# V mixed one column at a time: an attention-plus-feed-forward kernel on one Trainium2 core

## The chip, the cores and the metric

The kernel runs on one core of one Trainium2 chip. The metric is the device time of one execution in microseconds (us); of the kernel before, three runs are shown, with a median of 286.13 us (286.0 to 287.14). Engines are named as in the profile: PE is TensorE's matmul side and PEld its weight loads, DVE is VectorE, ACT is ScalarE, POOL is GpSimd, and SP is SyncE, which here only issues transfers. A matmul reads two operands from SBUF: the weights (`lhsT`), which are loaded first, and the moving operand (`rhs`), which is streamed past them. Both have the summed dimension on the partitions. The result has the weights' columns on its partitions and the moving columns along its rows, and lands in PSUM, from where DVE or ACT copies it to SBUF (an "eviction").

## What is computed

Four batches, 8 heads, 768 positions, 64 numbers per head; the positions form 8 blocks of 96. A small matrix per head, `sort_net` (8x8), is normalised five times over rows and columns, and then mixes the blocks of K and V. Attention is inside a block. The result goes through a gated feed-forward layer (512 to 1536 to 512).

```python
for _ in range(5):
    P = P - np.max(P, axis=-1, keepdims=True)
    P = np.exp(P)
    P = P / (np.sum(P, axis=-1, keepdims=True) + 1e-09)
    P = P / (np.sum(P, axis=-2, keepdims=True) + 1e-09)
k_sorted = np.einsum('bhij,bhjcd->bhicd', P, k_b)
v_sorted = np.einsum('bhij,bhjcd->bhicd', P, v_b)
scores = scale * (q_b @ k_sorted^T)          # per block of 96
attn = softmax(scores)
x = (attn @ v_sorted), heads side by side     # 3072 x 512
out = (silu(x @ w_gate) * (x @ w_val)) @ w_out
```

Here `j` is the block that is read, `i` the block that results, `c` the position in a block (96), `d` the number in a head (64). The attention needs, for each head and block `i`, the mixed V with its keys `c` on the partitions: that is the tile `vt` (96 partitions, 64 pairs of head and block, 64 numbers).

## The kernel before

The work is cut into 8 units: half a batch each, 4 of the 8 blocks of all heads, 384 rows of the result. A unit's attention goes by pairs of heads (`hp`, four per unit): `qk` (scores, tile `s`), `rowmax`, `shift`, `expo`, `rowsum`, `norm` (tile `en`), `turn` (the normalised weights are transposed on PE, tile `et`), `av` (they meet `vt`, and the result is evicted to `xt`). A unit's feed-forward has 12 steps: `ffn_up` (two times 4 matmuls, `g_ps` and `u_ps`, and a tanh on ACT), `ffn_gate` (DVE), and `ffn_down` of the unit before (`o_ps`, 3 of 12 matmuls per step). The feed-forward of a unit overlaps the attention of the next one.

Preparation, once per batch: Q is transposed on PE in 3 pieces (`q_piece`), K is mixed and transposed in 6 (`k_piece`, by `mix_t`), V is mixed in 6 (`v_piece`).

The order is written out by hand. Each step is put into a list with a due time in feed-forward steps, the list is sorted, and each engine runs its instructions in that order; a step that waits holds up whatever stands behind it on its engine. `prep` (L366) gives the due times of the pieces: batch 1's fall into the feed-forward of unit 0, batch 2's and 3's into that of the units 1, 2 and 3, 4. For the first unit there is a list of its own (`first`, L399), which runs ahead of all feed-forward steps.

V takes two ways:

- Batch 0: `load_v` puts V on 128 partitions, 16 per head: block `j` and half `ch` of the block, with 48 positions of 64 numbers along the row. `v0_piece` mixes it as `k_piece` mixes K: 6 pieces of 16 matmuls, of 64 weight columns (the numbers `d` at one position) and 64 moving columns (from `bdk`, a block-diagonal form of the mixing matrix). That leaves `d` on the partitions (`vT`). `v0_turn` then transposes on PE: 8 groups of 4 transposes (`vt_ps`), each evicted by ACT. The six pieces and eight turns are spread over `first` and the steps right behind it.
- Batches 1 to 3: `v_piece` is one matmul with `bdk` as weights and 512 moving columns of V, so the mixed V has head, block and half on the partitions (tile `vm`). `v_turn` writes it to a scratch tensor in DRAM with a transfer issued by SP and reads it back with keys on the partitions with a second one, in runs of 128 bytes. SP also issues the stores of the result.

All pieces of a batch after the first use the PSUM tag "m", a ring of two buffers shared with `turn` and `av`; the first unit's use "up", a ring of three, later used by `g_ps` and `u_ps`. ACT evicts all pieces of batches 1 to 3.

`bdk` comes out of the normalised matrix so: `spread_p` multiplies a 0/1 selection (`selk`) with it, which repeats each head's rows on its 16 partitions; `make_zk` keeps each partition's own column with a mask (`mjk`) and a sum; `make_bdk` spreads the outcome into the block-diagonal form with a second mask (`m1`). The masks are made on DVE and POOL during the five rounds. Loads of Q, K, V and the weights are issued by POOL (`load_q`, `load_k`, `load_v`, `load_w`) and convert to bf16 on the way.

```python
nc.tensor.matmul(ps.rearrange("p c d -> p (c d)"),          # v_piece
                 lhsT=bdk[:, b].rearrange("p h i c -> p (h i c)"),
                 rhs=vn[b][:, ts(n, 8), :].rearrange("p c d -> p (c d)"))
```

The functions that the change touches and what calls them, with the line numbers that the profile uses:

Of the kernel before, what the change touches and what calls it, by code (L numbers as in the profile page):

```python
# [9 lines left out]
FP32 = mybir.dt.float32  # L10
BF16 = mybir.dt.bfloat16
AF = mybir.ActivationFunctionType
ALU = mybir.AluOpType
AX = mybir.AxisListType
# [3 lines left out]
def kernel(  # L18
# [8 lines left out]
    moe_w_out: bass.AP,  # L27
    out: bass.AP,
):

    nc = tc.nc

    B, H, S, D = q.shape
    NB = sort_net.shape[-1]
# [12 lines left out]
    CH = 2  # L55
# [11 lines left out]
    hpool = ctx.enter_context(tc.tile_pool(name="hpool", bufs=2))  # L67
    gsp = ctx.enter_context(tc.tile_pool(name="gsp", bufs=3))
    opool = ctx.enter_context(tc.tile_pool(name="opool", bufs=3))
    dramp = ctx.enter_context(tc.tile_pool(name="dramp", bufs=2, space=bass.MemoryType.DRAM))  # L70
    psum = ctx.enter_context(tc.tile_pool(name="psum", bufs=2, space=bass.MemoryType.PSUM))

    def ps_tile(shape, dt, name, tag):
        return psum.tile(shape, dt, name=name, tag=tag, bufs={"up": 3, "o": 1, "s": 1, "m": 2}[tag])
# [17 lines left out]
        nc.gpsimd.dma_start(out=qn[b], in_=src)  # L92

    def load_v(b):
        vn[b] = natp.tile([128, CK, D], BF16, name="vn", tag="vn", bufs=2)
        src = v[b].rearrange("h (j ch c) d -> (h j ch) c d", j=NB, ch=CH)
        nc.gpsimd.dma_start(out=vn[b], in_=src)

    def load_w(dst, w, f0, f1):
        src = w.rearrange("(x hp d) f -> x d hp f", x=2, hp=HP)  # L100
# [17 lines left out]
    def evict(eng, dst, src):  # L118
        if eng == "act":
            nc.scalar.copy(dst, src)  # L120
        else:
            nc.vector.tensor_copy(dst, src)
# [11 lines left out]
    def mix_t(nat, b, dst, n, eng, tag):  # L134

        ps = ps_tile([128, 8, 64], FP32, "k_ps", tag)
        for l in range(8):
            for x in range(2):
                nc.tensor.matmul(ps[ds(64 * x, 64), l, :], lhsT=nat[:, n * 8 + l, :],  # L139
                                 rhs=bdk[:, b, ds(HP * x, HP)].rearrange("p a i c -> p (a i c)"),  # L140
                                 start=True, stop=True)
        dst = dst.rearrange("p hp i (ch c) -> p (hp i ch) c", ch=CH)
        evict(eng, dst[:, :, ts(n, 8)], ps.transpose([0, 2, 1]))
# [3 lines left out]
            tr["k", b] = trp.tile([128, HP, NB, BLK], BF16, name="kt", tag="kt")  # L147
        mix_t(kn[b], b, tr["k", b], n, eng, tag)

    def v0_piece(n, eng, tag):  # L150

        if n == 0:
            tr["vT"] = natp.tile([128, HP, NB, BLK], BF16, name="vT")
            tr["v", 0] = trp.tile([BLK, H * NB, D], BF16, name="vt", tag="vt")
        mix_t(vn[0], 0, tr["vT"], n, eng, tag)

    def v0_turn(hp, half, eng, tag):
        ps = ps_tile([BLK, HB, 2, D], BF16, "vt_ps", tag)
        for i in range(HB):
            nc.tensor.transpose(ps[:, i].rearrange("p x d -> p (x d)"),  # L160
                                tr["vT"][:, hp, half * HB + i, :], ident)
        dst = tr["v", 0].rearrange("p (x hp i) d -> p hp i x d", x=2, hp=HP)
        evict(eng, dst[:, hp, ds(half * HB, HB)], ps)

    def v_piece(b, n, eng, tag):
        if n == 0:
            tr["vm", b] = natp.tile([128, CK, D], BF16, name="vm", tag="vm", bufs=2)
        ps = ps_tile([128, 8, D], FP32, "v_ps", tag)
        nc.tensor.matmul(ps.rearrange("p c d -> p (c d)"),
                         lhsT=bdk[:, b].rearrange("p h i c -> p (h i c)"),  # L170
                         rhs=vn[b][:, ts(n, 8), :].rearrange("p c d -> p (c d)"),
                         start=True, stop=True)
        evict(eng, tr["vm", b][:, ts(n, 8), :], ps)

    def v_turn(b):
        scr = dramp.tile([H * NB, BLK, D], BF16, name="vscr", tag="vscr")
        nc.sync.dma_start(out=scr.rearrange("hi (ch c) d -> (hi ch) c d", ch=CH), in_=tr["vm", b])
        tr["v", b] = trp.tile([BLK, H * NB, D], BF16, name="vt", tag="vt")
        nc.sync.dma_start(out=tr["v", b], in_=scr.rearrange("hi c d -> c hi d"))


    nc.vector.memset(p_sb[:, NB:NB + 1, :], 1e-9)
    P = p_sb[:, 0:NB, :]
# [5 lines left out]
    for it in range(N_ITER):  # L189
        nc.scalar.activation(P, P, AF.Exp)  # L190
        nc.vector.reduce_sum(rowred[:, :, 0], P, axis=AX.X)
        nc.vector.reciprocal(rowred, rowred)
        nc.vector.tensor_mul(P, P, rowred.to_broadcast([BH, NB, NB]))
        nc.vector.reduce_sum(colred[:, 0, :], p_sb.transpose([0, 2, 1]), axis=AX.X)
        nc.vector.reciprocal(colred, colred)
        nc.vector.tensor_mul(pbf if it == N_ITER - 1 else P, P,
                             colred.to_broadcast([BH, NB, NB]))
        if it == N_ITER - 2:
            q_piece(0, 0, "act", "m")
        if it == N_ITER - 1:  # L200
            q_piece(0, 1, "act", "m")
            q_piece(0, 2, "act", "o")
        if it == 0:

            selk = const.tile([BH, BH, 16], BF16, name="selk")
            nc.gpsimd.tensor_copy(selk, ident[0:BH, 0:BH].unsqueeze(2).to_broadcast([BH, BH, 16]))
        if it == 1:
            mjk = const.tile([128, 1, NB], FP32, name="mjk")
            nc.vector.reduce_sum(mjk[:, 0, :], ident.rearrange("p (h j ch) -> p j h ch", j=NB, ch=CH),
                                 axis=AX.XY)  # L210
        if it == 2:
            m1 = const.tile([128, 8, CH], FP32, name="m1")
            nc.vector.reduce_sum(m1, ident.rearrange("p (h j ch) -> p h ch j", j=NB, ch=CH), axis=AX.X)


    zkr = const.tile([128, B, NB], FP32, name="zkr")
# [2 lines left out]
    def spread_p(b0, b1):  # L219
        ps = ps_tile([128, b1 - b0, NB, NB], FP32, "zk_ps", "up")  # L220
        for b in range(b0, b1):
            nc.tensor.matmul(ps[:, b - b0].rearrange("p i j -> p (i j)"),
                             lhsT=selk[:, ds(b * H, H), :].rearrange("p h r -> p (h r)"),
                             rhs=pbf.rearrange("p i j -> p (i j)"), start=True, stop=True)
        return ps

    def make_zk(b0, b1, ps):
        n = (b1 - b0) * NB
        zk = const.tile([128, n, NB], FP32, name=f"zk{b0}")
        nc.vector.tensor_tensor(zk, ps.rearrange("p b i j -> p (b i) j"),  # L230
                                mjk.to_broadcast([128, n, NB]), op=ALU.mult)
        nc.vector.reduce_sum(zkr[:, b0:b1, :].rearrange("p b i -> p (b i)"), zk, axis=AX.X)

    def make_bdk(b, eng):
        eng.tensor_tensor(
            bdk[:, b],
            m1.unsqueeze(2).to_broadcast([128, H, NB, CH]),
            zkr[:, b, :].unsqueeze(1).unsqueeze(3).to_broadcast([128, H, NB, CH]),
            op=ALU.mult)
# [120 lines left out]
    def at(t, f, *args):  # L360
        steps.append((t, lambda: f(*args)))
# [2 lines left out]
        nc.gpsimd.dma_start(out=wo_sb, in_=moe_w_out.rearrange("(mc p) f -> p mc f", p=128))  # L364

    def prep(b, tv, tk, tq, *engs):  # L366

        n = 0
        for f, times in [(v_piece, tv), (k_piece, tk), (q_piece, tq)]:
            for i, t in enumerate(times):  # L370
                at(t, f, b, i, engs[n % len(engs)], "m")
                n += 1
        at(tv[-1] + 0.3, v_turn, b)

    T0 = -15.6
    load_v(1)
    load_k(1)
    zk_ps = spread_p(0, 1), spread_p(1, B)
    make_zk(0, 1, zk_ps[0])
    make_bdk(0, nc.vector)  # L380
    for n in range(6):
        k_piece(0, n, ("dve", "act")[n % 2], ("m", "up", "m", "up", "m", "o")[n])
    make_zk(1, B, zk_ps[1])
# [4 lines left out]
    load_q(1)  # L388


    def v0(*ns):
        for n in ns:
            v0_piece(n, "act", "up")

    def vx(half, *hps):
        for hp in hps:
            v0_turn(hp, half, "act", "up")

    first = [(qk, 0), (rowmax, 0), (v0, 0, 1, 2), (shift, 0), (expo, 0), (qk, 1), (rowmax, 1),  # L399
             (v0, 3, 4), (shift, 1), (expo, 1), (v0, 5), (rowsum, 0), (norm, 0), (qk, 2),  # L400
             (rowmax, 2), (vx, 0, 0, 1), (shift, 2), (expo, 2), (rowsum, 1), (norm, 1),
             (vx, 0, 2, 3), (qk, 3), (turn, 0), (rowmax, 3), (shift, 3), (expo, 3), (av, 0),
             (turn, 1), (rowsum, 2), (norm, 2), (av, 1), (rowsum, 3),
             (norm, 3, (nc.vector, nc.gpsimd)), (vx, 1, 0, 1)]
    for f, *args in first:
        f(*args) if f in (v0, vx) else f(0, *args)
    at(T0 + 11.9, turn, 0, 2)
    at(T0 + 12.15, av, 0, 2)
    at(T0 + 12.7, turn, 0, 3)
    at(T0 + 13.0, av, 0, 3)  # L410
    at(T0 + 13.05, vx, 1, 2, 3)

    at(0.1, load_wo)
    at(2.1, load_v, 2)
# [2 lines left out]
    at(15.1, load_v, 3)  # L417
    at(17.1, load_k, 3)
    at(19.1, load_q, 3)
    prep(1, [0.45 + 0.5 * n for n in range(6)], [3.45 + 0.6 * n for n in range(6)],  # L420
         [7.2, 8.0, 8.8], "act")
    for b in range(2, B):
        t = 24 * (b - 2) + 12.45
        prep(b, [t + n for n in range(6)], [t + 6 + n for n in range(6)],
             [t + 12 + 2 * n for n in range(3)], "act")
    for u in range(1, NU):
        steps += att_steps(u, 12 * u + T0 + (u == 2))
# [39 lines left out]
```

## Time and profile before

| what | value |
|---|---|
| median of the runs shown | 286.13 us (286.0, 286.13, 287.14) |
| the profiled execution: span from its first to its last instruction | 284.0 us |
| PE busy | 258.5 us (91%) |
| DVE busy | 204.0 us (72%) |
| ACT busy | 164.3 us (58%) |
| POOL busy | 70.3 us (25%) |
| V, batch 0: `vT` matmuls (L139), turns (L160) on PE | 3.0 and 4.1 us |
| V, batch 0: evictions of `vT` and `vt` on ACT | 3.2 and 4.3 us |
| V, batches 1 to 3: 18 matmuls (L169), 18 evictions to `vm` | 6.8 and 10.4 us |
| V, batches 1 to 3: DRAM trip, issue to landing, medians | 6.7 out, 8.3 back |

The page gives, for the profiled execution, the busy time of each engine, the busy tenths in 40 slices of 7.1 us, the transfers, the chain of work that ended last, and the costliest groups of instructions. Of the execution's own time the profile has the span only; the median of the runs is 2.1 us longer. In a group, "busy" is the time in which at least one of its instructions ran and "mean ns" is that of one, so for overlapping matmuls the mean is longer than the distance between two starts. How long PE needs for a group is read from the order of time instead: the start of the next group less its own.

### The profile page before, as it was taken

How to read it: one execution, taken by the hardware profiler on the slowest of the kernel's cores; microseconds unless marked ns; L12 is line 12 of the kernel's file. 1: busy time of each engine (PE TensorE's matmuls, PEld its weight loads, DVE VectorE, ACT ScalarE, POOL GpSimd, SP SyncE). 2: the span in 40 equal slices, each digit the busy share in tenths (PEclk: the TensorE clock that was granted, in tenths of full speed). 3: DMA queues.
4: the chain of work that ended last, by engine and by line, in shares of the span. 5: the costliest groups of instructions: out<-in, count | busy, mean ns of one | idle time of the engine just before them, and what ended most of it. 6: DMA issues, size and time to landing. Idle time of an engine off the chain costs nothing.

```text
span 284.0 us, 6237 instructions
## 1 busy us (share of the span) xinstructions
PE 258.5 (91%) x2550; PEld 154.6 (54%) x2550; DVE 204.0 (72%) x360; ACT 164.3 (58%) x291; POOL 70.3 (25%) x98
## 2 busy tenths in 40 slices
PE   0577789989999999999999999999999999999983
PEld 0566645655556665555555655555555555555531
DVE  5789577749778777888887777888888887556500
ACT  2568779885766767546666666554555445432311
POOL 8155362433332222222211222222222222000000
PEclk9955589999999999999999999999999999999999
DMA  6999999997399911001039100101000010000021
GB/s 105 216 206 221 204 203 197 268 207 75 51 227 244 111 39 38 10 31 39 28 137 133 39 2 37 40 0 39 38 37 2 37 39 37 18 22 37 37 76 74
DMA packets 28412, 25.57 MB, mean 90 GB/s; under 512 B 19296, under 2 KB 22880, under 8 KB 28384
## 3 DMA queue, kind: packets, MB, share of 16 engines
q0 software_dynamic: 5968, 14.16, 26.7%
q1 hardware_dynamic: 22416, 11.02, 15.9%
q8 instruction: 20, 0.33, 0.5%
q14 instruction: 8, 0.07, 0.1%
HBM read 30.68 MB, written 8.65 MB: 138 GB/s over the span
## 4 chain that ended last, share of the span: by engine, by line
PE 65%; DVE 15%; ACT 12%; issue 4%; DMA 2%; DVEq 0%; ACTq 0%; POOLq 0%
PE o_ps L346 19%; PE g_ps L318 17%; PE u_ps L318 14%; DVE e L262 5%; DVE rm L257 5%; PE av_ps L298 3%; ACT et L120 3%; PE k_ps L139 3%; ACT e L267 3%; PE et_ps L285 2%; DMA qn<-in_q_dram 2%; ACT th L328 2%; PE s L251 2%; DVE gs L332 2%; DVE h L338 2%
## 5 line engine op out<-in xcount | busy, mean ns | idle before, releaser
L278 POOL TENSOR_TENSOR en<-e,rs 96x384 bf16<-96x384 f32 x63 | 50.9, 827 | 145.3 <-DVE rs L272 113.1
L332 DVE SCALAR_TENSOR_TENSOR gs<-th,g_ps 128x384 bf16<-128x384 bf16 x96 | 52.2, 544 | 42.5 <-ACT th L328 42.5
L346 PE MATMUL o_ps<-wo_sb,h 128*128 128x512 bf16 x288 | 76.8, 380 | 2.3 <-ACT o_sb L350 2.0
L318 PE MATMUL u_ps<-xt,wv_sb 128*128 128x384 bf16 x384 | 78.3, 327 | 0.6 <-DVE gs L332 0.5
L318 PE MATMUL g_ps<-xt,wg_sb 128*128 128x384 bf16 x384 | 78.8, 328 | 0.0
L328 ACT ACTIVATE th<-g_ps 128x384 bf16<-128x384 f32 x96 | 47.1, 490 | 53.9 <-PE g_ps L318 52.6
L338 DVE SCALAR_TENSOR_TENSOR h<-u_ps,gs 128x384 bf16<-128x384 f32 x92 | 51.3, 557 | 9.9 <-PE o_ps L346 0.5
L318 PEld LDWEIGHTS <-wg_sb 128*128 128x128 bf16 x384 | 36.9, 98 | 35.1 <-issue 2.0
L318 PEld LDWEIGHTS <-wv_sb 128*128 128x128 bf16 x384 | 37.7, 98 | 26.1 <-issue 1.6
L267 ACT ACTIVATE e<-e 96x768 f32<-96x768 f32 x32 | 27.0, 843 | 19.3 <-DVE e L262 19.3
L346 PEld LDWEIGHTS <-h 128*128 128x128 bf16 x288 | 23.9, 98 | 22.9 <-issue 3.1
L262 DVE TENSOR_TENSOR e<-s,rm 96x768 f32<-96x768 f32 x32 | 30.5, 954 | 2.8
L257 DVE TENSOR_REDUCE rm<-s 96x8 f32<-96x768 f32 x32 | 30.2, 943 | 2.8 <-PE s L251 2.7
L271 DVE TENSOR_REDUCE rs<-e 96x8 f32<-96x768 f32 x32 | 30.0, 938 | 1.3 <-ACT e L267 1.3
L120 ACT COPY et<-et_ps 96x768 bf16<-96x768 bf16 x32 | 25.0, 781 | 1.7 <-PE et_ps L285 1.7
L350 ACT COPY o_sb<-o_ps 128x512 f32<-128x512 f32 x24 | 14.0, 585 | 16.8 <-PE o_ps L346 16.7
L285 PEld LDWEIGHTS <-en 96*96 96x96 bf16 x256 | 17.4, 133 | 3.2
L285 PE MATMUL et_ps<-ident,en 96*96 96x96 bf16 x256 | 18.1, 217 | 0.0
L120 ACT CAST xt<-av_ps 128x384 bf16<-128x384 f32 x32 | 15.3, 477 | 4.4 <-PE av_ps L298 3.6
L130 PE MATMUL q_ps<-ident,qn 128*64 128x128 bf16 x192 | 8.5, 244 | 9.0 <-DMA qn<-in_q_dram 8.0
L298 PEld LDWEIGHTS <-vt 96*64 96x64 bf16 x256 | 9.4, 114 | 11.8 <-issue 11.3
L298 PE MATMUL av_ps<-et,vt 96*64 96x96 bf16 x256 | 12.2, 218 | 3.8 <-ACT et L120 3.3
(54 smaller groups left out, 154.3 us busy)
## 6 DMA issues: line engine op xcount, KB each, us to landing
out_dram<-o_sb SPq DMA_DIRECT2D x24, 256.0 KB, 2.0
qn<-in_q_dram POOLq DMA_DIRECT2D x4, 768.0 KB, 10.0
kn<-in_k_dram POOLq DMA_DIRECT2D x4, 768.0 KB, 10.4
vn<-in_v_dram POOLq DMA_DIRECT2D x4, 768.0 KB, 13.3
vscr<-vm SPq DMA_DIRECT2D x3, 768.0 KB, 6.7
vt<-vscr SPq DMA_DIRECT2D x3, 768.0 KB, 8.3
wg_sb<-in_moe_w_gate_dram POOLq DMA_DIRECT2D x4, 384.0 KB, 15.8
wv_sb<-in_moe_w_val_dram POOLq DMA_DIRECT2D x4, 384.0 KB, 18.1
```

Source lines behind the costliest of these rows:

```text
L120: nc.scalar.copy(dst, src)
L257: nc.vector.reduce_max(m[:, :, :, 0], st["s", u, hp], axis=AX.X)
L262: nc.vector.tensor_tensor(e, st["s", u, hp], st["m", u, hp].to_broadcast([BLK, 2, HB, BLK]), op=ALU.subtract)
L267: nc.scalar.activation(st["e", u, hp], st["e", u, hp], AF.Exp, scale=scale)
L278: engs[x].tensor_tensor(st["en", u, hp][:, x], st["e", u, hp][:, x], st["rs", u, hp][:, x].to_broadcast([BLK, HB, BLK]), op=ALU.mult)
L285: nc.tensor.transpose(ps[:, x * HB + i, :], st["en", u, hp][:, x, i, :], ident[0:BLK, 0:BLK])
L298: nc.tensor.matmul(ps[ds(64 * x, 64), i, :], lhsT=tr["v", b][:, (x * HP + hp) * NB + i0 + i, :], rhs=st["et", u, hp][:, x, i, :], start=Tr ...
L318: nc.tensor.matmul(ps, lhsT=w_sb[:, kc, ts(m, 128)], rhs=xt[u][:, kc, :], start=(kc == 0), stop=(kc == HP - 1))
L328: nc.scalar.activation(st["th"], st["g"], AF.Tanh, scale=0.5)
L332: nc.vector.scalar_tensor_tensor(gs, st["th"], 1.0, st["g"], op0=ALU.add, op1=ALU.mult)
L338: nc.vector.scalar_tensor_tensor(h_t[u][:, m, :], st["u"], 0.5, gs, op0=ALU.mult, op1=ALU.mult)
L346: nc.tensor.matmul(st["o"], lhsT=h_t[u][:, m, ts(t, 128)], rhs=wo_sb[:, m, :], start=(m == 0), stop=(m == NFC - 1))
```

## The change

V is loaded with each head's blocks on the partitions: partition (head, block `j`), 64 in all, and the whole block, 96 positions of 64 numbers, along the row. Two batches share one tile, the even one on partitions 0 to 63 and the odd one on 64 to 127. For mixing, the weights are one column `d` of V: 64 partitions and 96 positions, which lie 64 numbers (128 bytes) apart in SBUF. The moving operand is `pv`, the block-diagonal mixing matrix in a new form (64 partitions, 64 columns of head and block `i`). So each matmul gives, for one `d`, all heads' and blocks' mixed values with the keys on the partitions, which is the order that `av` reads. `pv` is made like `bdk`, by `spread_pv` and `make_pv` with the masks `selv`, `mjv` and `mhv`.

For batches 1 to 3, `v_piece` now has 8 matmuls (8 columns `d`), there are 8 pieces, and their eviction reads PSUM with a stride, as that of a K piece does. `v_turn` with its scratch tensor and its two transfers is gone. For batch 0, `v_half` makes 4 of the 8 blocks at a time (the half that one unit reads): 16 matmuls with 32 moving columns, two evictions by ACT of 256 numbers per partition; 4 pieces per half, 8 in all. `v0_piece`, `v0_turn` and `vT` are gone. The due times in `first` and `prep` change accordingly.

```diff
     def load_v(b):
-        vn[b] = natp.tile([128, CK, D], BF16, name="vn", tag="vn", bufs=2)
-        src = v[b].rearrange("h (j ch c) d -> (h j ch) c d", j=NB, ch=CH)
-        nc.gpsimd.dma_start(out=vn[b], in_=src)
+        if b % 2 == 0:
+            vn[b] = natp.tile([128, BLK, D], BF16, name="vn", tag="vn", bufs=2)
+            vn[b + 1] = vn[b]
+        nc.gpsimd.dma_start(out=vn[b][ds(64 * (b % 2), 64)],
+                            in_=v[b].rearrange("h (j c) d -> (h j) c d", j=NB))
...
-    def v0_piece(n, eng, tag):
...
-    def v0_turn(hp, half, eng, tag):
...
+    def v_half(b, half, n, eng, tag):
+
+        if half == 0 and n == 0:
+            tr["v", b] = trp.tile([BLK, H * NB, D], BF16, name="vt", tag="vt")
+        r = ds(64 * (b % 2), 64)
+        ps = ps_tile([BLK, 16, H, HB], FP32, "v_ps", tag)
+        for l in range(16):
+            nc.tensor.matmul(ps[:, l], lhsT=vn[b][r, :, n * 16 + l],
+                             rhs=pv[r, b // 2, :, ds(half * HB, HB)], start=True, stop=True)
+        dst = tr["v", b].rearrange("p (h i) d -> p h i d", h=H)
+        for l in range(2):
+            evict(eng, dst[:, ds(l * HP, HP), ds(half * HB, HB), ts(n, 16)],
+                  ps[:, :, ds(l * HP, HP)].transpose([0, 2, 3, 1]))
 
     def v_piece(b, n, eng, tag):
         if n == 0:
-            tr["vm", b] = natp.tile([128, CK, D], BF16, name="vm", tag="vm", bufs=2)
-        ps = ps_tile([128, 8, D], FP32, "v_ps", tag)
-        nc.tensor.matmul(ps.rearrange("p c d -> p (c d)"),
-                         lhsT=bdk[:, b].rearrange("p h i c -> p (h i c)"),
-                         rhs=vn[b][:, ts(n, 8), :].rearrange("p c d -> p (c d)"),
-                         start=True, stop=True)
-        evict(eng, tr["vm", b][:, ts(n, 8), :], ps)
-
-    def v_turn(b):
...
+            tr["v", b] = trp.tile([BLK, H * NB, D], BF16, name="vt", tag="vt")
+        r = ds(64 * (b % 2), 64)
+        ps = ps_tile([BLK, 8, H * NB], FP32, "v_ps", tag)
+        for l in range(8):
+            nc.tensor.matmul(ps[:, l], lhsT=vn[b][r, :, n * 8 + l],
+                             rhs=pv[r, b // 2].rearrange("p h i -> p (h i)"), start=True, stop=True)
+        evict(eng, tr["v", b][:, :, ts(n, 8)], ps.transpose([0, 2, 1]))
...
+            selv = const.tile([BH, BH, NB], BF16, name="selv")
+            nc.gpsimd.tensor_copy(selv, ident[0:BH, 0:BH].unsqueeze(2).to_broadcast([BH, BH, NB]))
...
+        if it == 3:
+
+            mjv = const.tile([128, 1, NB], FP32, name="mjv")
+            nc.vector.reduce_sum(mjv[:, 0, :], ident.rearrange("p (b h j) -> p j b h", b=2, j=NB), axis=AX.XY)
+            mhv = const.tile([128, H], FP32, name="mhv")
+            nc.vector.reduce_sum(mhv, ident.rearrange("p (b h j) -> p h b j", b=2, j=NB), axis=AX.XY)
...
+    def spread_pv(tag):
+        ps = ps_tile([128, B // 2, NB, NB], FP32, "zv_ps", tag)
+        for b2 in range(B // 2):
+            nc.tensor.matmul(ps[:, b2].rearrange("p i j -> p (i j)"),
+                             lhsT=selv[:, ds(b2 * 2 * H, 2 * H), :].rearrange("p h r -> p (h r)"),
+                             rhs=pbf.rearrange("p i j -> p (i j)"), start=True, stop=True)
+        return ps
+
+    def make_pv(ps):
+        n = B // 2 * NB
+        zv = const.tile([128, n, NB], FP32, name="zv")
+        nc.vector.tensor_tensor(zv, ps.rearrange("p b i j -> p (b i) j"),
+                                mjv.to_broadcast([128, n, NB]), op=ALU.mult)
+        nc.vector.reduce_sum(zvr.rearrange("p b i -> p (b i)"), zv, axis=AX.X)
+        for b2 in range(B // 2):
+            nc.gpsimd.tensor_tensor(pv[:, b2], mhv.unsqueeze(2).to_broadcast([128, H, NB]),
+                                    zvr[:, b2, :].unsqueeze(1).to_broadcast([128, H, NB]), op=ALU.mult)
...
-        at(tv[-1] + 0.3, v_turn, b)
...
     zk_ps = spread_p(0, 1), spread_p(1, B)
+    zv_ps = spread_pv("up")
     make_zk(0, 1, zk_ps[0])
     make_bdk(0, nc.vector)
+    make_pv(zv_ps)
...
+    first = [(qk, 0), (rowmax, 0), (vh, 0, 0, 1), (shift, 0), (expo, 0), (qk, 1), (rowmax, 1),
+             (vh, 0, 2), (shift, 1), (expo, 1), (vh, 0, 3), (rowsum, 0), (norm, 0), (qk, 2),
+             (rowmax, 2), (shift, 2), (expo, 2), (rowsum, 1), (norm, 1), (vh, 1, 0),
+             (qk, 3), (turn, 0), (rowmax, 3), (shift, 3), (expo, 3), (av, 0),
+             (turn, 1), (rowsum, 2), (norm, 2), (av, 1), (rowsum, 3),
+             (norm, 3, (nc.vector, nc.gpsimd)), (vh, 1, 1)]
...
-    at(T0 + 13.05, vx, 1, 2, 3)
+    at(T0 + 13.05, vh, 1, 2, 3)
...
-    prep(1, [0.45 + 0.5 * n for n in range(6)], [3.45 + 0.6 * n for n in range(6)],
+    prep(1, [0.45 + 0.4 * n for n in range(8)], [3.45 + 0.6 * n for n in range(6)],
          [7.2, 8.0, 8.8], "act")
...
-        prep(b, [t + n for n in range(6)], [t + 6 + n for n in range(6)],
+        prep(b, [t + 0.75 * n for n in range(8)], [t + 6 + n for n in range(6)],
              [t + 12 + 2 * n for n in range(3)], "act")
```

## The prediction

> **What bounds the kernel now.** I read first the busy tenths and the granted clock over the span:
>
> ```profile
> PE   0577789989999999999999999999999999999983
> PEclk9955589999999999999999999999999999999999
> ```
>
> TensorE (PE) is full from about 62 us on; before that there is a stretch at half clock. The stretches, with each engine's busy time (PE, PEld, DVE, ACT, POOL), granted clock and DMA:
>
> ```profile
> 16.00:36.40 20.40, 15.07 (x241) 13.29 (x241) 15.46 (x22) 15.61 (x27) 10.26 (x15) 0.50 1.12 211
> 36.40:62.00 25.60, 23.03 (x304) 14.38 (x302) 16.99 (x28) 21.09 (x38) 12.02 (x15) 0.97 1.11 220
> 125.00:145.00 20.00, 19.93 (x158) 11.04 (x158) 15.86 (x28) 12.31 (x25) 4.82 (x6) 1.00 0.08 31
> ```
>
> These are three regimes: the first unit at half clock (16 to 36 us), where PE, DVE and ACT take turns; a mixed one (36 to 62), in which batch 1's preparation falls, ACT 82% busy and PE 90%; then PE alone. A modelled matmul end can hide a gap, so I went to the order of time for a v piece of batch 2 and its neighbours (start, us, line):
>
> ```profile
> 69.55 0.81 PE L318 MATMUL u_ps<-xt,wv_sb 128*128 128x384 bf16 x4
> 70.20 0.52 PE L285 MATMUL et_ps<-ident,en 96*96 96x96 bf16 x8
> 70.56 0.38 PE L169 MATMUL v_ps<-vn,bdk 128*128 128x512 bf16 x1
> 70.78 0.81 PE L346 MATMUL o_ps<-wo_sb,h 128*128 128x512 bf16 x3
> ...
> 72.08 0.81 PE L318 MATMUL u_ps<-xt,wv_sb 128*128 128x384 bf16 x4
> 72.82 0.36 PE L298 MATMUL av_ps<-et,vt 96*64 96x96 bf16 x8
> ```
>
> Read the differences of the starts. u_ps takes 0.65 (69.55 to 70.20), as every u_ps ahead of an et_ps from 62 to 245 us does: nothing waits. et_ps takes 0.36 for 8, 45 ns each, with a 96-column weight load for every 96 columns streamed. The old v piece takes 0.22. u_ps ahead of av_ps takes 0.74: 0.09 more on entering a form that uses half the array, and the same stands ahead of s. Inside an s group the pairs start 45 ns apart and the last is followed after 0.13. So from 62 to 270 us whatever PE gets more is paid in time.
>
> Two rows serve as a price of reading SBUF with a stride:
>
> ```profile
> L194 DVE TENSOR_REDUCE colred<-p_sb x5: 266/268/270, 3.8 to 11.0; 32x8 f32<-32x72 f32 x5
> L191 DVE TENSOR_REDUCE rowred<-p_sb x5: 207/207/208, 3.1 to 10.3; 32x8 f32<-32x64 f32 x5
> ```
>
> rowred reads consecutive numbers; colred reads 72 with 32 bytes from one to the next. At 1.05 ns an element (96x768 rm 943 ns less rowred's 207, over 704) the 8 more explain 8 of the 61 ns; 53 over 72 leaves 0.73 ns an element, 1.7 times the price of a consecutive one.
>
> **The change, batches 2 and 3.** Removed per batch: 6 v pieces of 0.22 = 1.3 us of PE; 6 ACT evictions (588 ns); two SP transfers. Those hide nothing that matters: the mixed V of batch 1 lands at 68.5 and is read at about 73, later batches have tens of us; no PE wait names them. So the DRAM trip gives 0, and SP's output stores behind it (one issue held 6 us) free no PE either.
>
> Added per batch: 8 pieces of 8 matmuls, each with its own load of 96 weight columns, 128 bytes apart, and 64 columns streamed. All 8 use the same 64 rows, so none runs beside another. The pitch is not in the trace. Lower end: 32 ns, the pair pitch of k_ps (64 columns loaded, 64 streamed). With a load of 96 consecutive columns et_ps says 45. Upper end: 40 ns of the 45 are columns (o_ps streams 512 in 0.217 us, so 96 in 40 ns); if each costs what colred's elements cost outright (1.78 ns), 176. I take 40 x 1.7 + 5 = 73 ns: et_ps is the nearest form, colred the only row that reads one element per stride. A piece is then 0.09 to enter + 7 x 0.073 + 0.13 to leave = 0.73; eight 5.9; in batch 2 two pieces are due right behind an s group, a half-array form too, and save 0.19 each: 5.5. Net of 1.3: +4.2 us and +4.6 us, all on PE, **+8.8** for the two. With 45 ns it is +5.6, with 32 ns +4.1. ACT's two more evictions (96x512 out of PSUM by stride; kt, the same pattern, took 584 ns against vm's 588) lie beside PE; ACT is 62% busy there.
>
> [...]
>
> **Batch 1, 36 to 62 us.** The same +4.2 of PE and +1.2 of ACT (two of 584). PE lost 1.4 us there waiting to reuse the two "m" buffers ahead of v pieces (0.9 behind et's copy, 0.25 behind xt's); longer pieces use that up. Bounds: 45 ns and all waits absorbed, +1.2; nothing absorbed and ACT's 1.2 added, +5.4. I take **+3.5**.
>
> **Batch 0, 13 to 38 us.** DVE: make_pv's two instructions (0.23 to 0.28 each, after zk and zkr 128x64) fall into the 0.63 that DVE waited for the first k_ps; mjv and mhv (0.27 each, as mjk) into its 0.48 wait for ACT in the last round, about 0.05 beyond. Without those covers 1.1 in all. PE: 2 spread matmuls, 0.1, while bdk is made. POOL: a selv copy (under selk's 0.64) ahead of load_v(1), and two pv products (0.4 each, as bdk) in its 7.5 us idle; load_w and q(1), queued behind, wait for transfers anyway. The "up" ring has one tile more; its slots are freed by make_zk and make_pv. V lands on 64 partitions: the weights' 384 KB pieces, also 64 partitions, landed about 2.1 us apart against 3.6 for 768 KB on 128; so 4.2, landing 0.6 later than 15.2, read from 16.5: hidden.
>
> Removed on PE: 96 matmuls (3.0 us busy) and 32 transposes (4.1), at half clock:
>
> ```profile
> 29.04 0.53 PE L298 MATMUL av_ps<-et,vt 96*64 96x96 bf16 x8 [0.99 <-ACT et L120]
> 29.50 1.09 PE L160 MATMUL vt_ps<-ident,vT 128*96 128x128 bf16 x8
> 30.39 0.85 PE L285 MATMUL et_ps<-ident,en 96*96 96x96 bf16 x8
> ...
> 34.85 1.09 PE L160 MATMUL vt_ps<-ident,vT 128*96 128x128 bf16 x8
> 35.87 0.56 PE L251 MATMUL s<-kt,qt 64*96 64x96 bf16 x8
> ```
>
> Added: 8 halves of 16 matmuls, 96 columns loaded, 32 streamed. At half clock a column is asked for every 0.83 ns, slower than the 0.71 (40 x 1.7 / 96) assumed above, so 80 ns each, as et_ps's starts lie apart at half clock; 1.3 a half. (Lower end 27, the 32 streamed columns alone; upper 136, 1.7 times.) Before qk 1 there are now two halves, 2.6, where three pieces took 1.5: PE reaches qk 1 at 19.1 instead of 18.56. Halves 2 and 3 put qk 2 at 22.1 instead of 21.15; DVE's row sums fill part of it, and by av 1 0.3 is left. From there PE and ACT alternate: one half for 8 transposes +0.4 (1.3 for 0.9), two ahead of qk(1,1) +1.6 (2.6 for 1.0). ACT has 16 evictions of 256 (0.37 by the slope from 477 at 384 to 584 at 512), 5.9, for 14 that took 7.5 (vT 3.2, vt 4.3); that relief lies where ACT isn't last. That is +2.3. [...] **+3.0**, between -1.5 (27 ns) and +8 (136 ns, 7.2 us more, two thirds of it on the path).
>
> **Sum:** 284.0 + 8.8 + 3.5 + 3.0 = 299.3 us of span. The median of the runs is 286.13, 2.1 above this execution's span, which is all that the profile has of its time; I leave that 2.1 around it: 301.4 us.
>
> **Rivals.** (a) The strided load costs no more than a consecutive one, 45 ns: 5.6 + 2 + 3 = +10.6, 296.7. For it: a weight load starts while the matmul before it runs, and strides out of PSUM cost ACT nothing. Against: PSUM is not SBUF, and colred paid.
> (b) The pieces lie beside the DVE and ACT chain, not on PE: not slower. The chain of waits runs through them even late:
>
> ```profile
> 114.44 0.87 DVE rm L257
> 115.40 0.96 DVE e L262
> 117.23 0.69 ACT et L120
> ```
>
> Then batches 1 to 3 add nothing, batch 0 gains 1.5 from ACT's lighter copies: 284.6. It decides if PE idles 4.2 us in six feed-forward steps; against it, the starts leave under 0.1 per step.
> (c) The clock returns early, near 21 us, because PE is fuller in the first unit. Its later chain (5.2 us of PE at half clock) would shrink by 2.6 and g, u by 0.8: with (a) and halves that no longer cost more than what they replace, 290 to 292.
> (d) It is far worse: loads at 176 ns, or batch 0's mixing waits for batch 1's V, now in the same tile and landing at 27.5: +10 on the first unit. Against the latter: the halves of wg_sb, one tile, are loaded without waiting for each other. 309 or more.
> (e) A load of 96 columns goes at the half-clock pace, 80 ns, whatever the stride: 302. Against it, et_ps made one every 45 ns. [...]
>
> **How the numbers follow.** My case, 298 to 308: 0.46; (e) inside it: 0.04. (a), 293 to 298: 0.32. (c), 288 to 293: 0.06. (b): 0.05. (d): 0.07. The range 291.5 to 308 leaves out (d), (b) and part of (c), 0.16. A measurement tells 0.5% (1.4 us) from no change: slower 0.93, the same 0.02, faster 0.05, the last two from (b) and the best of (c).
>
> **What would show it.** Starts of the new v_ps groups in batches 2 and 3: 0.6 to 0.75 us per piece of 8 and 73 ns between matmuls confirm my case, 45 ns (a). PE without gaps from 62 us on, otherwise (b). In the first unit: 80 ns at half clock; g_ps first at about 39 instead of 36.4; clock 0.5 as before, otherwise (c). The prediction is wrong above all if the pitch is.

## The result and the profile after

The changed kernel takes 335.25 us (median of four runs, 334.54 to 338.62); the kernel before took 286.33 us beside it (286.0 to 287.14). The ratio is 1.173, with a 95% interval of 1.167 to 1.179. It is slower, as forecast, but by 49 us where 15 were forecast, and the time lies outside the range. The profiled execution has a span of 333.7 us, 49.7 more than that of before.

The page of the kernel after, busy time per engine and the busy tenths of PE (40 slices of 8.3 us):

```profile
PE 310.2 (93%) x2726; PEld 202.7 (61%) x2726; DVE 206.9 (62%) x364; ACT 167.2 (50%) x299; POOL 71.1 (21%) x101
PE   0798889999899999999999999999999999999984
```

PE has 51.7 us more busy time (258.5 before), DVE and ACT under 3 more, so PE is where to look for the loss. To see in which part of the work, I cut both executions at the first `g_ps` of each unit and set the same stretches side by side. Kernel before, stretches of the trace (start:end, length, busy time of PE, PEld, DVE, ACT, POOL, then granted clock, DMA share, GB/s): the first unit's attention, and the feed-forward of units 0, 1 and 3:

```profile
16.00:36.40 20.40, 15.07 (x241) 13.29 (x241) 15.46 (x22) 15.61 (x27) 10.26 (x15) 0.50 1.12 211
36.40:66.10 29.70, 26.59 (x336) 16.37 (x335) 20.85 (x34) 23.51 (x43) 12.02 (x15) 0.97 1.16 214
66.10:98.40 32.30, 32.23 (x339) 18.63 (x338) 26.00 (x44) 21.54 (x41) 10.70 (x14) 1.00 0.81 145
128.40:160.20 31.80, 31.78 (x332) 18.37 (x331) 24.87 (x42) 21.13 (x39) 6.43 (x8) 1.00 0.37 76
```

Kernel after, the same four stretches:

```profile
16.00:49.10 33.10, 29.12 (x256) 28.20 (x252) 17.09 (x24) 14.07 (x31) 12.85 (x18) 1.00 0.86 161
49.10:94.10 45.00, 42.97 (x394) 29.34 (x394) 21.17 (x34) 25.29 (x46) 9.36 (x12) 0.89 0.51 88
94.10:136.90 42.80, 42.73 (x398) 28.41 (x397) 26.41 (x44) 23.19 (x43) 10.70 (x14) 1.00 0.35 69
166.90:209.10 42.20, 42.20 (x390) 28.44 (x389) 24.96 (x42) 22.77 (x41) 6.42 (x8) 1.00 0.05 20
```

The loss is in the four stretches in which V is mixed: 12.7, 15.3, 10.5 and 10.4 us. Units 2, 4, 5, 6 and 7 together grew by 0.8. In units 1 and 3 PE stands idle for under 0.1 us before and after, so the growth there is PE work. (The clock's 1.00 in the first row of after and part of its 0.89 in the second aren't readings: the trace has no clock record before 63.8 us there. The distances of the matmuls tell it: up to 63.8 us `et_ps` start 80 ns apart and `g_ps` 320, as where 0.5 is recorded; at a recorded 1.0 it is 45 and 163.)

Now the order of time on PE in the kernel after (start, duration, line). The first rows are the first unit, the next batch 1 at half clock, the last batch 2 at full clock:

```profile
36.13 2.80 PE L152 MATMUL v_ps<-pv,vn 64*96 64x32 bf16 x16
38.86 0.87 PE L301 MATMUL et_ps<-ident,en 96*96 96x96 bf16 x8
39.66 0.56 PE L267 MATMUL s<-kt,qt 64*96 64x96 bf16 x8
...
69.38 1.49 PE L334 MATMUL u_ps<-xt,wv_sb 128*128 128x384 bf16 x4
70.80 1.52 PE L165 MATMUL v_ps<-pv,vn 64*96 64x64 bf16 x8
72.25 0.87 PE L301 MATMUL et_ps<-ident,en 96*96 96x96 bf16 x8
...
98.58 0.81 PE L334 MATMUL u_ps<-xt,wv_sb 128*128 128x384 bf16 x4
99.32 1.49 PE L165 MATMUL v_ps<-pv,vn 64*96 64x64 bf16 x8
100.74 0.56 PE L301 MATMUL et_ps<-ident,en 96*96 96x96 bf16 x8
```

A piece of 8 takes 1.42 us at full clock (99.32 to 100.74) and 1.45 at half clock (70.80 to 72.25); a half of 16, with half as many columns streamed, 2.73 (36.13 to 38.86). Inside the groups the single matmuls start 163 to 165 ns apart in all three, behind a first step of 185 or 186. Neither the columns streamed (32 or 64) nor the clock matters, while `et_ps` beside them goes from 45 to 80 ns a matmul. That points to the weight load as what sets the pitch, at 1.70 ns per strided column (163 over 96); the first two experiments test it. The groups of the page agree:

```profile
L165 PEld LDWEIGHTS <-vn 64*96 64x96 bf16 x192 | 33.0, 251 | 6.8 <-issue 6.5
L165 PE MATMUL v_ps<-pv,vn 64*96 64x64 bf16 x192 | 35.2, 330 | 0.2 <-ACT vt L115 0.2
L152 PE MATMUL v_ps<-pv,vn 64*96 64x32 bf16 x128 | 21.7, 320 | 0.0
```

These matmuls are 56.9 us of PE, for the 13.9 (3.0, 4.1 and 6.8) that they replace. The evictions are not in the way (PE waited 0.2 us for one, once).

### The profile page after: what moved, and what is told of

Read it like the earlier page. It is cut to its first block, busy times and chain, and to the rows that moved or that the text cites. A ratio compares the mean times of both kernels' runs of the same rounds, so it can differ in the third digit from the quotient of the medians.

```text
span 333.7 us, 6594 instructions
## 1 busy us (share of the span) xinstructions
PE 310.2 (93%) x2726; PEld 202.7 (61%) x2726; DVE 206.9 (62%) x364; ACT 167.2 (50%) x299; POOL 71.1 (21%) x101
## 4 chain that ended last, share of the span: by engine, by line
PE 75%; DVE 12%; ACT 8%; issue 3%; DMA 1%; DVEq 0%; ACTq 0%
PE o_ps L362 17%; PE g_ps L334 16%; PE u_ps L334 14%; PE v_ps L165 10%; PE v_ps L152 5%; DVE e L278 3%; PE k_ps L134 3%; DVE rm L273 3%; PE et_ps L301 3%; PE av_ps L314 3%; ACT et L115 2%; PE s L267 2%; ACT e L283 2%; ACT th L344 2%; DVE gs L348 2%
## 5 line engine op out<-in xcount | busy, mean ns | idle before, releaser
L334 PE MATMUL u_ps<-xt,wv_sb 128*128 128x384 bf16 x384 | 81.4, 336 | 0.6 <-DVE gs L348 0.5
L334 PE MATMUL g_ps<-xt,wg_sb 128*128 128x384 bf16 x384 | 81.5, 336 | 0.0
L334 PEld LDWEIGHTS <-wv_sb 128*128 128x128 bf16 x384 | 38.6, 101 | 27.9 <-issue 4.6
L115 ACT CAST vt<-v_ps 96x512 bf16<-96x512 f32 (+1 forms) x40 | 19.1, 496 | 47.7 <-PE v_ps L165 33.3
L273 DVE TENSOR_REDUCE rm<-s 96x8 f32<-96x768 f32 x32 | 30.3, 945 | 16.0 <-PE s L267 15.9
L165 PEld LDWEIGHTS <-vn 64*96 64x96 bf16 x192 | 33.0, 251 | 6.8 <-issue 6.5
L362 PEld LDWEIGHTS <-h 128*128 128x128 bf16 x288 | 23.0, 97 | 21.9 <-issue 2.9
L165 PE MATMUL v_ps<-pv,vn 64*96 64x64 bf16 x192 | 35.2, 330 | 0.2 <-ACT vt L115 0.2
L152 PE MATMUL v_ps<-pv,vn 64*96 64x32 bf16 x128 | 21.7, 320 | 0.0
L152 PEld LDWEIGHTS <-vn 64*96 64x96 bf16 x128 | 21.4, 253 | 0.2
```

The lines of the kernel that those rows point to most:

```text
L152: nc.tensor.matmul(ps[:, l], lhsT=vn[b][r, :, n * 16 + l], rhs=pv[r, b // 2, :, ds(half * HB, HB)], start=True, stop=True)
L165: nc.tensor.matmul(ps[:, l], lhsT=vn[b][r, :, n * 8 + l], rhs=pv[r, b // 2].rearrange("p h i -> p (h i)"), start=True, stop=True)
L273: nc.vector.reduce_max(m[:, :, :, 0], st["s", u, hp], axis=AX.X)
L334: nc.tensor.matmul(ps, lhsT=w_sb[:, kc, ts(m, 128)], rhs=xt[u][:, kc, :], start=(kc == 0), stop=(kc == HP - 1))
L362: nc.tensor.matmul(st["o"], lhsT=h_t[u][:, m, ts(t, 128)], rhs=wo_sb[:, m, :], start=(m == 0), stop=(m == NFC - 1))
```

## The experiments

The theory was that the stride of the load is nearly the whole of the excess over the forecast; the rivals were that a load of 96 columns on 64 rows is slow however it reads, and that the number of matmuls, the clock or the first unit's order carry it. Where the expectations say "line", 16 bytes are meant; what bears that size out is the ladder below (177 ns a load at a step of 16 bytes, 180 and 164 beyond). Each is compared with the kernel before on the same chip (286.5 to 286.6 us).

**Consecutive weights.** The same matmuls, but each takes its 96 weights from consecutive numbers of V, and likewise in `v_half`.

```diff
-lhsT=vn[b][r, :, n * 8 + l]
+lhsT=vn[b][r].rearrange("p c d -> p (c d)")[:, ts(n * 8 + l, BLK)]
```

> Every V matmul of the changed kernel takes 96 consecutive numbers of V's tile as its weights instead of 96 that lie 128 bytes apart; everything else stays (so V is mixed from other numbers, and the output is not the reference's). Theory 'line': a weight column costs the read of the SBUF line that it lies in, 1.70 ns (163 ns over 96 columns in the changed kernel, at both clocks); with consecutive columns the starts in a v piece lie 45 ns apart, a piece takes about 0.55 us instead of 1.42, and the kernel 293 to 298 us. Rival 'row group': the loads cannot be made while a matmul streams, because all of a piece use the same 64 rows; then the stride is not it, the starts stay 163 ns apart and the kernel at 335 us.

Measured: 299.74 us (298.24 to 300.18), ratio 1.044 (1.041 to 1.047), span 298.4. The order of time on PE, first unit and batch 2:

```profile
30.29 1.46 PE L152 MATMUL v_ps<-pv,vn 64*96 64x32 bf16 x16
31.68 0.87 PE L301 MATMUL et_ps<-ident,en 96*96 96x96 bf16 x8
...
77.46 0.81 PE L334 MATMUL u_ps<-xt,wv_sb 128*128 128x384 bf16 x4
78.21 0.54 PE L165 MATMUL v_ps<-pv,vn 64*96 64x64 bf16 x8
78.68 0.56 PE L301 MATMUL et_ps<-ident,en 96*96 96x96 bf16 x8
```

A piece now takes 0.47 us (78.21 to 78.68) instead of 1.42, 45 ns a matmul, and a half 1.39 instead of 2.73. So 64 rows alone cost nothing more, and the stride costs 335.25 - 299.74 = 35.5 us of the 49, with what it does to the clock. The time is 1.7 us above the range that I expected. The other 13.2 us remain when the 320 small matmuls take consecutive weights: the first `g_ps` is 2.9 us later than before, unit 0 takes 4.9 us longer, units 1 and 3 2.9 each. The stretches of units 0 and 3:

```profile
39.20:73.90 34.70, 31.97 (x395) 21.03 (x394) 21.14 (x34) 24.93 (x46) 10.59 (x14) 1.00 0.71 126
139.10:173.80 34.70, 34.70 (x390) 20.95 (x389) 24.85 (x42) 22.61 (x41) 6.43 (x8) 1.00 0.07 24
```

In units 1 and 3, at full clock, the eight pieces take 3.7 to 3.8 us of PE for the 1.35 to 1.47 of the six old ones, which is most of the 2.9. In unit 0 it is not the pieces alone: the clock came back about 48 us here, 9 us into the unit, and 38 before, 1.6 into it (`g_ps` 320 ns apart until then; the 1.00 above counts stretches without a record). How much of the 4.9 that is was not measured by itself. The stride is therefore the larger part, not all: without it the change would still lose.

**A ladder of strides.** In batch 2 each of the eight pieces loads its 96 columns with another step between the numbers (1, 2, 3, 4, 6, 8, 16, 64); in batch 3 the step of the moving operand and the number of rows are changed instead, and behind the last step DVE, ACT and POOL each copy 96 numbers at six steps.

```diff
-            nc.tensor.matmul(ps[:, l], lhsT=vn[b][r, :, n * 8 + l],
-                             rhs=pv[r, b // 2].rearrange("p h i -> p (h i)"), start=True, stop=True)
...
+            wt = flat[:, 0:96 * sl].rearrange("p (c s) -> p c s", s=sl)[:, :, l % sl]
...
+            if sm:
+                mv = flat[:, 0:64 * sm].rearrange("p (c s) -> p c s", s=sm)[:, :, l % sm]
...
+                nc.tensor.matmul(ps[ds(c0, cn), l], lhsT=wt[:, ds(c0, cn)], rhs=mv, start=True, stop=True)
...
```

> One look at prices, by the starts inside the pieces. Batch 2's eight pieces load 96 columns at steps of 1, 2, 3, 4, 6, 8, 16 and 64 numbers (2 to 128 bytes); batch 3's take consecutive loads with 64 moving columns at steps of 1, 64, 8 and 4 numbers, then a strided load cut into 64 and 32 columns, a strided load on all 128 rows, a consecutive load on 128 rows, and that with strided moving columns. Behind the last store, DVE, ACT and POOL copy 96 numbers each at six steps. V of the batches 2 and 3 is not mixed rightly, so the output is not the reference's. Theory 'line' (a 16-byte line costs 1.70 ns, whatever is used of it): 45, 45, 64, 85, 125, 163, 163, 163 ns; 163 on 128 rows too; 64 and 32 columns 109 and 55; the moving side, if it reads the same way, 109, 109 and 54 ns at 64, 8 and 4. Rival 'two per line are enough': 45 ns up to a step of 4, then up. Rival 'row group': 163 ns at every step, less on 128 rows. Rival 'fixed price of such a load': 163 for 64 and for 32 columns.

Measured: 326.9 us in a single run, read here for its prices only. The order of time on PE, with the group that follows each piece, for the steps 1, 3, 4, 6 and 64:

```profile
91.99 0.51 PE L181 MATMUL v_ps<-pv,vn 64*96 64x64 bf16 x8
92.43 0.82 PE L377 MATMUL o_ps<-wo_sb,h 128*128 128x512 bf16 x3
...
96.10 0.72 PE L181 MATMUL v_ps<-pv,vn 64*96 64x64 bf16 x8
96.75 0.82 PE L349 MATMUL g_ps<-xt,wg_sb 128*128 128x384 bf16 x4
...
99.20 0.90 PE L181 MATMUL v_ps<-pv,vn 64*96 64x64 bf16 x8
100.04 0.82 PE L349 MATMUL g_ps<-xt,wg_sb 128*128 128x384 bf16 x4
...
101.66 1.21 PE L181 MATMUL v_ps<-pv,vn 64*96 64x64 bf16 x8
102.80 0.82 PE L377 MATMUL o_ps<-wo_sb,h 128*128 128x512 bf16 x3
...
111.51 1.49 PE L181 MATMUL v_ps<-pv,vn 64*96 64x64 bf16 x8
112.94 0.66 PE L349 MATMUL g_ps<-xt,wg_sb 128*128 128x384 bf16 x3
```

The groups take 0.44, 0.65, 0.84, 1.14 and 1.43 us. From the starts of the single matmuls, all at full clock:

| step of the load, numbers of 2 bytes | 1 | 2 | 3 | 4 | 6 | 8 | 16 | 64 |
|---|---|---|---|---|---|---|---|---|
| pitch of a 96-column matmul, ns | 45 | 47 | 68 | 90 | 133 | 177 | 180 | 164 |
| chunks of 16 bytes that 96 numbers touch | 12 | 24 | 36 | 48 | 72 | 96 | 96 | 96 |
| ns per 16 bytes touched | | 2.0 | 1.89 | 1.88 | 1.85 | 1.84 | 1.88 | 1.71 |

From 3 to 8 numbers (16 bytes) the price is proportional to the step (68 to 177 ns), and beyond it hardly rises (180 and 164): in this ladder a load cost 45 ns or about 1.85 ns for each 16 bytes that it touches, whichever is more. The 1.70 ns a line that I expected, taken from step 64, is a little low for the others; why step 64 is cheaper than 8 and 16 was not settled. The rivals "two per line are enough" and "row group" fall: at step 4 the price is 90 ns and not 45, and it is not 163 at every step. Batch 3: a moving operand read by stride pays too (64 columns at step 64: 111 ns, at step 8: 116, at step 4: 60, consecutive: 45). With 128 rows the load cost the same, 163 ns strided and 45 consecutive. A strided load split into 64 and 32 columns took 390 ns a pair, dearer than the 164 in one; I had expected 109 and 55, and a fixed price for each load would give twice 163; the starts lie 222 and 168 ns apart. The two halves also alternate between two shapes, and what of it costs so much was not settled.

The other engines forgive more. Their copies of 96 numbers, one copy at each of the steps 1, 2, 4, 8, 16 and 64: DVE 201, 206, 204, 237, 240, 234 ns; ACT 273, 272, 274, 358, 360, 350; POOL 259, 259, 259, 343, 348, 339. At step 4, two numbers in 16 bytes, these copies took what consecutive ones take (204 for 201, 274 for 273, 259 for 259 ns), while PE's loads took 90 ns instead of 45; there it took four numbers in 16 bytes (step 2, 47 ns) to come within 2 ns of a consecutive load.

**Halves of the change.** First batch 0 alone the old way, with batches 1 to 3 as in the change; then batch 0 as in the change, with batches 1 to 3 the old way, DRAM trip included.

```diff
-    def v_half(b, half, n, eng, tag):
...
+    def v0_piece(n, eng, tag):
...
+    def v0_turn(hp, half, eng, tag):
...
```

> The changed kernel with batch 0 in the way of before (its load, its six pieces, its eight turns, its order of the first unit); batches 1 to 3 as changed. If the added PE time is all there is, this gives back the delay of the first unit (first g_ps at 36.4 us instead of 49.1) and the half that lies in unit 0: 335 - 12.7 - 2.8 = about 320 us. If the first unit's delay had been hidden later, it stays near 335.

```diff
...
+    def v_turn(b):
...
+        at(tv[-1] + 0.3, v_turn, b)
...
-    prep(1, [0.45 + 0.4 * n for n in range(8)], [3.45 + 0.6 * n for n in range(6)],
+    prep(1, [0.45 + 0.5 * n for n in range(6)], [3.45 + 0.6 * n for n in range(6)],
```

> The changed kernel with batches 1 to 3 in the way of before (six pieces each and the trip through DRAM); batch 0 as changed. If PE time adds up one to one, the three batches give back 3 x 10.5 us, and about 2 us of half clock in unit 0 may go with them: 301 to 304 us, and units 1 and 3 last 29.7 to 32.3 us as before. If the removed DRAM trip had been worth something, more than 304.

Measured: 324.2 us (323.02 to 325.38; ratio 1.131, 1.126 to 1.136) and 299.35 us (299.15 to 299.55; 1.044, 1.042 to 1.047). Batch 0's part is thus +12.8 us, that of batches 1 to 3 +37.7; the sum, 50.5, is within 2 us of the 48.9 of both together. I expected 4 us less of the first kernel. Of that 2.8 were a misreading: I had a half left over behind the first `g_ps`, where the trace has all eight ahead of it; another 1.6 are a longer unit 3 (below). The second kernel is 1.7 us faster than the range that I expected: unit 0 gave back 14.7 us (30.3 instead of 45.0), where I had 12.5. Units 1 and 3 take 32.6 and 31.75 us there, as before (32.3, 31.8). With the DRAM trip in place PE is busy in unit 3 for 31.78 of 31.80 us and in unit 1 for 32.23 of 32.30 (the last two rows of before, above), so there was no wait for the trip that its removal could have saved.

**K ahead of V in batch 1.** Unit 0 grew by 15.2 us, of which PE's starts put 7.6 on the V pieces; 7.7 lie on `g_ps`, `u_ps` and the other groups, at half clock for some 25 us. If the strided pieces merely came too early, while the clock was still low, putting K's pieces first (batch 0 the old way, as above) should give that back. The rival put on record was that the loss is waits for the "m" buffers and ACT.

```diff
-    prep(1, [0.45 + 0.4 * n for n in range(8)], [3.45 + 0.6 * n for n in range(6)],
+    prep(1, [3.7 + 0.4 * n for n in range(8)], [0.45 + 0.5 * n for n in range(6)],
```

> The kernel with batch 0 in the way of before and batches 1 to 3 as changed (324.2 us, first g_ps at 36.9, clock back at 65.0 instead of 38.0), with one thing moved: batch 1's K pieces are due ahead of its V pieces (K from 0.45, V from 3.7 feed-forward steps). Theory 'clock': the strided loads leave PE streaming so little that the granted clock stays at half through unit 0; with the dense steps and K pieces first, it returns within two windows of 3.4 us (before 46 us), unit 0 lasts 4 to 6 us less than 45.2, and the kernel takes 318 to 321 us. Rival: the 4.9 us that unit 0 lost beyond the pieces' own 10.5 are waits for the "m" buffers and ACT; then the order matters little, 323 to 326.

Measured: 324.38 us (322.24 and 326.53), no different from the 324.2 with V first. The time is the rival's, but not its reason: PE stands idle for 2.5 us in unit 0, where it was 3.1 in the kernel before. The clock record has it back at 41.3 us, ahead of the 46 that the theory gave (3.4 us is a length that the traces show: in the clock records of the kernels before and after the stretches last 3.41, 10.24 and 23.89 us, one, three and seven times 3.41); it fell again from 54.9 to 65.2 and from 68.6 to 75.4, while the V pieces ran from 48.5 to 67.9; unit 0 took 45.0 us, as it did with V first (45.2). So the pieces did not merely come too early: with the clock back in full it fell again among them and just behind them. Something like it shows in unit 3, where three kernels do identical work. With batch 0 the old way:

```profile
154.90:198.70 43.80, 43.80 (x390) 28.98 (x389) 25.02 (x42) 22.79 (x41) 6.43 (x8) 0.96 0.05 19
```

With K ahead of V as well:

```profile
154.70:199.90 45.20, 45.20 (x390) 29.35 (x389) 25.09 (x42) 22.78 (x41) 6.42 (x8) 0.92 0.05 18
```

Beside the 42.20 at 1.00 of the kernel after, they have one and two stretches of 3.4 us at half clock, and each costs about 1.5 us. Neither the kernel before nor the one with consecutive weights has such a stretch in unit 3. So within unit 3 the granted clock came down only where strided pieces run, and not in every execution (not in that of the kernel after); by what rule, these runs don't say.

**Keeping the clock up.** Rival (c) gave a price to an early clock in the first unit. To measure it by itself, the kernel before gets matmuls that nobody reads (128x512, `ident` as weights) in PE's idle times there: 41 in one version, 20 in the other.

```diff
+    def fill(n):
+        ps = ps_tile([128, 512], FP32, "w_ps", "o")
+        for _ in range(n):
+            nc.tensor.matmul(ps, lhsT=ident, rhs=qn[0].rearrange("p x c d -> p (x c d)")[:, 0:512],
+                             start=True, stop=True)
...
-    first = [(qk, 0), (rowmax, 0), (v0, 0, 1, 2), (shift, 0), (expo, 0), (qk, 1), (rowmax, 1),
+    first = [(fill, 3), (qk, 0), (rowmax, 0), (v0, 0, 1, 2), (shift, 0), (expo, 0), (fill, 4), (qk, 1), (rowmax, 1),
...
```

> The kernel before, with matmuls added in the first unit whose results nobody reads: 9 while the mixing matrix is made, and 2 to 4 of 512 columns where PE stands waiting (ahead of the score groups, the turns of V and each av): 41 in all. Theory 'clock': if they keep PE streaming, the clock is granted in full from about 14 to 38 us, PE's part of the first unit's later chain (about 5 us at half clock) halves, and the kernel takes 282 to 285 us. Rival: they delay what is behind them, at half clock 0.43 us each, and the clock stays: 288 to 296 us.

> The same with about half as many added matmuls (5 first, then 1 or 2 a place, 20 in all), which fit into PE's waits even at half clock. Theory 'clock': returns for part of the first unit, 284 to 286 us. Rival: too few to bring the clock back, and nothing is gained: 286 to 288.

Measured: 288.06 us (ratio 1.0037, 1.0013 to 1.0060) and 286.32 us (1.0004, 0.998 to 1.003). The stretch of the first with 41:

```profile
16.00:36.90 20.90, 16.96 (x279) 10.48 (x273) 15.74 (x23) 15.53 (x28) 10.25 (x15) 1.00 1.12 211
```

It is at full clock from 11.4 us on, and the first `g_ps` still comes at 36.9 instead of 36.4; DVE (15.74) and ACT (15.53) are as busy as before. The filling ahead of them puts the first scores off by 1.55 us (17.52 instead of 15.97), so the way from there to the first `g_ps` is only 1.0 us shorter, with the other added matmuls still in it. Unit 0 takes 30.2, 0.5 more than before. So the gain of rival (c) was not to be had in this way; what an early clock without the added matmuls would be worth isn't measured. Both times lie where the rival put them, but in both the clock did come back early (with 20, full from 17.7 to 31.4 us and half again up to 38.2).

## Why the prediction was right or wrong

- **PE bounds everything from 62 us on, and what PE gets more is paid in time: right.** Units 1 and 3 grew by 10.5 each, without a gap; the eight pieces take 11.3 to 11.4 of PE for the 1.35 to 1.47 of the six old ones. Rival (b), no loss beside the DVE and ACT chain, falls.
- **"I take 40 x 1.7 + 5 = 73 ns: et_ps is the nearest form": wrong, and this is the step that failed.** It measured 163. Of `colred` I used the ratio of its stride to a consecutive read and carried that over to PE's faster columns. The ladder's prices are not a factor on PE's own rate but, from step 3 on, 1.7 to 1.9 ns for each 16 bytes touched, and at 128 bytes the same at both clocks (163 ns). `colred`'s price outright, 1.78 ns an element, which I had as the upper end, was within 5% of the 1.70 measured, but nothing here shows that to be more than luck: DVE's own copies paid only 33 to 39 ns for the stride over 96 numbers, 0.4 ns each. Terms: batches 2 and 3 +21.0 instead of +8.8.
- **First unit, +3.0: wrong by the same step,** +12.7. A half takes 2.73 us instead of 1.3, since "slower than the 0.71 assumed above" rested on the 73 ns. With consecutive weights the rest of that working holds: 1.39 a half, and the first `g_ps` 2.9 us later, at 39.2 where about 39 was forecast. Not all of the 12.7 is the change's: in this execution the first scores already start 1.1 us later than before (17.06, 15.97), while the ladder kernel, which has the same instructions up to there, starts them at 15.94.
- **Batch 1, +3.5, and the clock (+0.7, inside the first unit's +3.0): wrong,** +15.2. By the pieces alone it would be about 7.6, again the pitch; the other 7.7 lie on groups at a half clock that lasted through most of unit 0. The 0.7 was an estimate of mine that no run shows; what they showed is a clock back in full 14.7 us into unit 0 (at 63.8 us) and at half again from 67.2 to 77.4, where before it came back 1.6 into it. With consecutive weights the term is +4.9, above the 3.5 taken and inside its bounds (1.2 to 5.4), but that too has some 7 us more of half clock in it, which the bounds had no term for.
- **The three terms together** miss by 12.2 + 9.7 + 11.7 = 33.6 us, which is the distance from 301.4 to 335.25 within 0.3.
- **Rival (d) had the right condition (loads at 176 ns), but neither its time nor its chance.** "309 or more" was not worked out. With 176 ns in the prediction's own sums, a piece is 0.09 + 7 x 0.176 + 0.13 = 1.45 and eight 11.6: batches 2 and 3 +20.2, batch 1 some +10; in the first unit 128 matmuls are 96 ns dearer than at 80, 12.3 us, two thirds on the path, so 3.0 + 8.2 = +11.2. That is 284 + 20.2 + 10 + 11.2 + 2.1 = 327.5, and the clock in unit 0 is most of what remains. The only row in the trace that read one element per stride pointed there; it deserved more than 0.07, and the range should have reached it. Its other condition did not occur: PE's first V matmul follows the first scores at 17.3 us, with no wait for a load.
- **Rival (a), no price for the stride, falls by 35 us,** though its terms are nearly what consecutive weights gave: 296.7 worked out, 299.74 measured.
- **Rival (c), the clock back near 21 us, did not occur:** from 31 to 41 us `et_ps` start 80 ns apart, as at half clock.
- **Rival (e), 80 ns for 96 columns whatever the stride, falls:** at full clock the ladder has 45 ns at step 1 and 164 at step 64.
- **What was costed at nothing shows no cost:** the DRAM trip (PE is full with it and without it), V's load on 64 partitions (no PE wait names it), ACT's two more evictions per batch (one PE wait of 0.2 us).

## What to carry to other kernels

Count the chunks of 16 bytes that a matmul's operand touches: in the ladder PE paid 1.7 to 1.9 ns for each from step 3 on, so 96 bf16 weights read 128 bytes apart cost 164 ns instead of 45, and at half clock 163. A layout that saves a transpose or a trip through DRAM by reading an operand with a stride can move more work than that into PE's loads (56.9 us of PE for 13.9 here); if the trip lay beside a full PE, as it did here (31.78 of 31.80 us in unit 3), its removal wins nothing back. When a price is unknown, carry over the nearest row's absolute time as well as its ratio, and give the case that follows its worked-out time and a real chance.

## What the runs showed of the hardware that was not expected

- A 96-column load's pitch against its step is level up to 2 numbers, then a straight line up to a knee at 16 bytes: 45, 47, 68, 90, 133, 177 ns at 1, 2, 3, 4, 6, 8 numbers, then 180 and 164 at 16 and 64.
- The pitch of a load at step 64 is the same at half clock (163 ns), while that of `et_ps`, with consecutive loads, goes from 45 to 80.
- The moving operand paid for a stride too: 111 ns for 64 columns at step 64, 1.73 ns each, and 45 consecutive.
- DVE, ACT and POOL read two numbers per 16 bytes at no extra cost (204, 274 and 259 ns for 96, consecutive 201, 273 and 259); at one per 16 bytes 96 numbers cost them 33 to 39, 77 to 87 and 80 to 89 ns more.
- Among strided pieces the granted clock can fall in the middle of a full PE: stretches of 3.4 us at half clock that cost about 1.5 us each, none, one or two in the same work. A full clock bought with 41 added matmuls in the first unit gained nothing (288.06 us, 286.6 before).
